# Output by seven half products in four steps of six instead of two, and earlier places for the v loads of the second sequence

## The chip, the cores and the metric

The kernel runs on one core of a Trainium2 chip. The metric is the device time of one execution in microseconds (us); the median of a few runs is compared. The engines of the core are called PE (TensorE), DVE (VectorE), ACT (ScalarE), POOL (GpSimd) and SP (SyncE, which here only issues transfers).

## What is computed

Eight sequences of 3072 tokens with 256 channels go through a gated attention without softmax, and the result through a feed-forward layer that takes the larger of two products:

```python
scores = (1.0 / S) * np.matmul(z, z.transpose(0, 2, 1))   # z: 8 x 3072 x 64
attn = np.maximum(scores, 0.0) ** 2
x = u * np.matmul(attn, v)                                # u, v: 8 x 3072 x 256
h1, h2 = x @ w1, x @ w2                                   # w1, w2: 256 x 1024
out = np.maximum(h1, h2) @ w_out                          # w_out: 1024 x 256
```

The scores of a sequence are symmetric, so the kernel computes a block once and lets the transfer engines transpose it for the other use.

## The kernel before

**Steps.** A sequence is cut into six groups of 512 tokens; a step is one group of output tokens. There are 48 steps: step n belongs to sequence b = n // 6 and has the number s = n % 6 in it. `SEVEN`, the constant of the change, is a set of such numbers s.

**One step on PE** is, in order: the output product of the step three before (`put_o`), the products X and Y of attention with v, and among them the four pairs of banks of the first feed-forward product (`put_d`) of the step two before, and scores of steps to come. Attention times v is done with seven products in place of eight (a Strassen-Winograd scheme): X and Y are sums of such products, their operands are sums over score tiles (`es`, made by DVE in `S1` to `S4`) and over v (`lf`, made by DVE in the jobs `fold`). Most matmuls run as two halves of 64 rows next to each other (`halved`, line 99).

**Scores.** A pair of score tiles goes from PE to a relu (mostly ACT, line 276) and a square (ACT, line 282, or DVE, line 284). SP then issues its transposition `aT<-a_sb`, called a turn, so that a later step can use the block from the other side. X of a step reads turned tiles of all earlier steps of the sequence; the last of them are made in the step just before.

**The output product.** `w_out` times g, g being the larger of the two hidden products. It is written here in two ways:

- *Plain* (`add_second`): four blocks of 128 tokens, ten products each of 64 rows twice, 80 matmuls of 64x256. Two copies by ACT (`oc`, line 287), then the store.
- *Seven* (`add_seven`, line 924; for steps with `s in SEVEN`): seven half products of whole rows, 72 matmuls of 128x128. DVE makes three operand tiles and changes one in place (`G3`, `G1`, `G2`, `G4`, each 128x1024) before the product, and adds the parts after it (`oA` to `oF`: four of 128x256, two of 128x512). ACT copies once 128x256 and once 128x512 (`oc0`, `oc1`).

**The order** of every engine is written by the program when it is built. The order of PE is laid out by hand in `work`. For the other engines a list scheduler (`find_orders`) plays the jobs against a table of costs, with due times from PE's order, 24 rounds, and keeps the round that ends PE first; it decides which squares go to ACT or DVE and in what order SP issues the turns, the transposition of u (`uT`) and the stores. So a changed job changes the order of all the engines around it.

**Loads** are issued by POOL in program order, each timed by a place on PE. v comes in six loads of 256 KB per sequence (`add_v`, line 344), two to a pair buffer; there are six pair buffers, and a sequence uses three. `v_at` (line 1541 for sequence 1, line 1544 for the others) gives their places as (step s, us after its start) in the sequence before; `quiet` (line 1477) moves a place that lies in step 3 or later to the next quiet spot of PE's order. Beside the loads, POOL writes small marks (line 95) that order the two halves of a bank.

Of the kernel before, what the change touches and what calls it, by code (L numbers as in the profile page):

```python
# [11 lines left out]
def kernel(  # L12
# [38 lines left out]
    NDIAG = 2  # L51
    PLAIN = 3
    NA, NT, WIDE = 16, 18, 19
    SEVEN = (0, 1)
    SEVEN_FROM, SEVEN_TO = 0, 46
    SPARE_D = (46, 2)
    DIAG_LAG = 8700, 6700
# [177 lines left out]
    class Step:  # L235
        def __init__(self, n, b, s):
# [3 lines left out]
            self.parted = 0 < n < B * NG - LAG + 1  # L240
            self.seven = s in SEVEN and SEVEN_FROM <= n < SEVEN_TO
            self.count = [0] * KD
# [76 lines left out]
    def v_order(b):  # L319
        return [1, 2, 3, 4, 5, 0] if b else list(range(NG))  # L320
# [23 lines left out]
    def add_v(b, g, at):  # L344
        first = v_pair(b, g)[1] == 0
        if first:
            buf(*v_key(b, g), lambda: vpool.tile([P, 2, G, D], bf16, name="v_sb"))

        def fetch(_):
            load(  # L350
                timed=at is not None,
                out=v_tile(b, g),
                in_=v[b].rearrange("(p t) d -> p t d", p=P)[:, ds(g * G, G), :],
            )

        job(
            ("v", b, g),
            {"POOL": 1300},
            fetch,
            new=v_key(b, g) if first else None,  # L360
            uses=[v_key(b, g)],
            after=list(at or ()) + ([] if first else [("v", b, v_order(b)[v_order(b).index(g) - 1])]),
            lag=8000,
        )
# [1104 lines left out]
    def at_step(b, s, us):  # L1469
        return pe_job_at(starts[NG * b + s] + us * 1000)  # L1470
# [6 lines left out]
    def quiet(at):  # L1477
        i = pe_order.index(at[0])
        if pe_at[i] < starts[LAG]:
            return at  # L1480
        found = [key for key in pe_order[i:] if key in QUIET]
        return found[:1] or at
# [32 lines left out]
    def add_z(b, at, turn_at):  # L1515
        def fetch(_):
            load(
                timed=True,
                out=z_sb_0[:, 1 : 1 + NSB, :],
                in_=z[b].rearrange("(p t) d -> p t d", p=P),  # L1520
            )

        def turn_z(_):
            seqs[b].zT = make_zT(z_sb_0)

        job(("z", b), {"POOL": 1800}, fetch, after=at, lag=7500)
        job(("zT", b), {"SP": 3500}, turn_z, deps=[("z", b)], after=turn_at, lag=3500)
# [10 lines left out]
    for b in range(1, B):  # L1538
        if b == 1:
            z_at, zT_at = (2, 6), (3, 2)  # L1540
            v_at = [(3, 16), (4, 4), (4, 9), (4, 14), (5, 0), (5, 4)]
        else:
            z_at, zT_at = (2, 9), (3, 4)
            v_at = [(3, 11), (3, 16), (4, 5), (4, 12), (5, 2), (5, 6)]
        add_z(b, quiet(at_step(b - 1, *z_at)), at_step(b - 1, *zT_at))
        for g, at in zip(v_order(b), v_at):
            add_v(b, g, quiet(at_step(b - 1, *at)))
# [424 lines left out]
```

## Time and profile before

| what | value |
|---|---|
| runs shown | 915.99, 916.46, 918.47 us, median 916.46 us |
| profiled execution | 915.38 us, of which the span is 913.4 us |
| busy: PE, DVE, ACT, POOL | 901.6, 756.3, 665.1, 92.1 us |
| granted TensorE clock, mean | 0.998 |
| moved by transfers | 146.31 MB, mean 160 GB/s |

The span is the time from the first to the last instruction of one execution. Busy times are the union of an engine's instructions. PE means matmuls, PEld the loading of weights, which overlaps them.

### The profile page before, as it was taken

How to read it: one execution, taken by the hardware profiler on the slowest of the kernel's cores; microseconds unless marked ns; L12 is line 12 of the kernel's file. 1: busy time of each engine (PE TensorE's matmuls, PEld its weight loads, DVE VectorE, ACT ScalarE, POOL GpSimd, SP SyncE). 2: the span in 40 equal slices, each digit the busy share in tenths (PEclk: the TensorE clock that was granted, in tenths of full speed). 3: DMA queues.
4: the chain of work that ended last, by engine and by line, in shares of the span. 5: the costliest groups of instructions: out<-in, count | busy, mean ns of one | idle time of the engine just before them, and what ended most of it. 6: DMA issues, size and time to landing. Idle time of an engine off the chain costs nothing.

```text
span 913.4 us, 31836 instructions
## 1 busy us (share of the span) xinstructions
PE 901.6 (99%) x13685; PEld 672.2 (74%) x13685; DVE 756.3 (83%) x1485; ACT 665.1 (73%) x811; POOL 92.1 (10%) x447
## 2 busy tenths in 40 slices
PE   8999799999999999999999999999999999999998
PEld 3367577777777777777777877778777887777775
DVE  6888688898888988889887998779987899888951
ACT  8868687578776778677786777866888568875634
POOL 2101100111001110011100011000100011000000
PEclk9999999999999999999999999999999999999999
DMA  9999999999999999999999999999999999997711
GB/s 155 169 154 176 167 175 185 168 164 191 177 160 163 149 177 173 167 167 160 165 170 177 147 188 156 179 167 162 161 170 160 174 143 181 188 157 114 123 60 70
DMA packets 382909, 146.31 MB, mean 160 GB/s; under 512 B 361264, under 2 KB 362928, under 8 KB 382768
## 3 DMA queue, kind: packets, MB, share of 16 engines
q1 hardware_dynamic: 366208, 114.54, 75.1%
q0 software_dynamic: 16560, 29.74, 24.1%
q8 instruction: 107, 1.75, 0.8%
q14 instruction: 34, 0.28, 0.1%
HBM read 59.77 MB, written 25.17 MB: 93 GB/s over the span
## 4 chain that ended last, share of the span: by engine, by line
PE 93%; ACT 2%; DMA 2%; DVE 1%; issue 0%; POOL 0%; SPq 0%; POOLq 0%; DVEq 0%
PE acc L87 47%; PE s_ps L87 46%; ACT a_sb L276 1%; DMA v_sb<-in_v_dram 1%; DMA aT<-a_sb 1%; ACT a_held L276 0%; DVE es L290 0%; PE zeros L87 0%; ACT g_sb L276 0%; ACT a_sb L282 0%; DVE e L290 0%; DVE a_sb L293 0%; DVE es L293 0%; DVE xT L297 0%; PE tpz_c L130 0%
## 5 line engine op out<-in xcount | busy, mean ns | idle before, releaser
L87 PEld LDWEIGHTS <-v_sb 64*128 64x128 bf16 (+1 forms) x4464 | 307.7, 94 | 81.9 <-POOL mark_sb L95 15.5
L276 ACT ACTIVATE a_sb<-s_ps 128x1024 bf16<-128x1024 f32 x337 | 301.6, 942 | 83.0 <-PE s_ps L87 80.8
L87 PEld LDWEIGHTS <-lf 64*128 64x128 bf16 x3240 | 246.7, 94 | 49.3 <-POOL mark_sb L95 15.5
L87 PE MATMUL acc<-es,v_sb 64*128 64x256 bf16 x2160 | 279.0, 269 | 0.0
L87 PE MATMUL acc<-es,lf 64*128 64x256 bf16 x1080 | 247.6, 269 | 0.0
L87 PE MATMUL acc<-a_sb,lf 64*128 64x256 bf16 x1224 | 227.1, 269 | 0.4 <-DVE e L290 0.4
L284 DVE TENSOR_TENSOR a_sb<-a_sb 128x1024 bf16<-128x1024 bf16 (+1 forms) x209 | 134.6, 655 | 79.0 <-ACT a_sb L276 73.6
L276 ACT ACTIVATE g_sb<-s_ps 128x1024 bf16<-128x1024 f32 x187 | 185.6, 1025 | 10.0 <-PE s_ps L87 9.4
L87 PE MATMUL s_ps<-xT,w_sb 64*128 64x512 bf16 (+1 forms) x1484 | 189.9, 377 | 0.3 <-POOL mark_sb L95 0.3
L87 PE MATMUL acc<-aT,lf 64*128 64x256 bf16 x936 | 174.1, 270 | 3.3 <-DMA aT<-a_sb 3.3
L87 PE MATMUL s_ps<-w_out_sb,g_sb 64*128 64x256 bf16 (+1 forms) x2240 | 145.6, 263 | 0.0
L290 DVE TENSOR_TENSOR e<-e,acc 128x512 f32<-128x512 f32 (+1 forms) x225 | 125.8, 575 | 19.6 <-PE acc L87 10.6
L87 PE MATMUL acc<-a_sb,v_sb 64*128 64x256 bf16 (+1 forms) x1352 | 140.9, 281 | 0.1
L87 PEld LDWEIGHTS <-g_sb 64*128 64x128 bf16 (+1 forms) x2496 | 126.5, 95 | 15.4 <-issue 3.8
L287 ACT COPY o_sb<-s_ps 128x512 f32<-128x512 f32 (+1 forms) x98 | 51.5, 543 | 106.4 <-PE s_ps L87 104.1
L87 PEld LDWEIGHTS <-w_sb 64*128 64x128 bf16 (+1 forms) x1488 | 69.3, 94 | 70.3 <-POOL mark_sb L95 30.0
L87 PE MATMUL s_ps<-zT 64*128 64x512 bf16 (+2 forms) x774 | 117.0, 334 | 0.4 <-DVE zT L131 0.3
L282 ACT ACTIVATE a_sb<-a_sb 128x1024 bf16<-128x1024 bf16 (+1 forms) x129 | 116.0, 921 | 1.3
L290 DVE TENSOR_TENSOR es<-aT 128x1536 bf16<-128x1536 bf16 (+1 forms) x117 | 106.9, 929 | 5.4 <-DMA aT<-a_sb 5.2
L95 POOL MEMSET mark_sb<- 128x1 bf16 x332 | 33.7, 102 | 720.8 <-PE acc L87 410.1
L87 PE MATMUL acc<-aT,v_sb 64*128 64x256 bf16 x936 | 85.1, 270 | 1.6 <-DMA aT<-a_sb 1.6
L293 DVE TENSOR_TENSOR es<-a_sb 128x512 bf16<-128x512 bf16 x198 | 80.1, 417 | 3.0 <-PE acc L87 2.5
(68 smaller groups left out, 724.4 us busy)
## 6 DMA issues: line engine op xcount, KB each, us to landing
out_dram<-o_sb SPq DMA_DIRECT2D x47, 512.0 KB, 5.9
v_sb<-in_v_dram POOLq DMA_DIRECT2D x48, 256.0 KB, 6.1
u_sb<-in_u_dram POOLq DMA_DIRECT2D x48, 256.0 KB, 5.5
aT<-a_sb SPq DMA_TRANSPOSE x230, 4.9
z_sb<-in_z_dram POOLq DMA_DIRECT2D x7, 384.0 KB, 5.1
w_sb<-in_moe_w_dram POOLq DMA_DIRECT2D x2, 512.0 KB, 7.0
uT<-u_sb SPq DMA_TRANSPOSE x48, 4.6
a_sb<-a_sb SPq DMA_TRANSPOSE x45, 5.6
```

What stands on the lines that cost most here:

```text
L87: newest[0] = pin(nc.tensor.matmul(*args, **kw)).ins
L95: ins = pin(nc.gpsimd.memset(mark_sb, 0.0)).ins
L276: pin(nc.scalar.activation(out_ap, in_ap, AF.Relu))
L282: pin(nc.scalar.activation(ap, ap, AF.Square))
L284: pin(nc.vector.tensor_mul(ap, ap, ap))
L287: pin(nc.scalar.copy(out_ap, in_ap) if eng == "ACT" else nc.vector.tensor_copy(out_ap, in_ap))
L290: pin(nc.vector.tensor_add(*args))
L293: pin(nc.vector.tensor_sub(*args))
```

## The change

Two constants are changed; the code is the same.

```diff
-    SEVEN = (0, 1)
+    SEVEN = (0, 1, 2, 4)
     SEVEN_FROM, SEVEN_TO = 0, 46
...
         if b == 1:
             z_at, zT_at = (2, 6), (3, 2)
-            v_at = [(3, 16), (4, 4), (4, 9), (4, 14), (5, 0), (5, 4)]
+            v_at = [(0, 8), (3, 12), (3, 16), (4, 4), (4, 8), (5, 4)]
```

With the first, 31 steps take the output product by seven half products instead of 16: those with s of 0, 1, 2 or 4 and n below 46. The fifteen new ones are steps 2 and 4 of the first sequence, both in the next six, and step 2 of the last.

With the second, the six loads of v for sequence 1 are issued at other places during sequence 0: the first in step 0, behind the load of w2, instead of late in step 3; the second and third together at the place that the first had; the fourth and fifth at the places that the second and third had; the last with the u load of step 6, as before.

## The prediction

> **What bounds the kernel now.** I read the page first, then PE's waits, the chain of waits, and the busy time by stage.
>
> ```profile
> span 913.4 us, 31836 instructions
> PE 901.6 (99%) x13685; PEld 672.2 (74%) x13685; DVE 756.3 (83%) x1485; ACT 665.1 (73%) x811; POOL 92.1 (10%) x447
> ...
> q1 hardware_dynamic: 366208, 114.54, 75.1%
> q0 software_dynamic: 16560, 29.74, 24.1%
> ...
> PE 93%; ACT 2%; DMA 2%; DVE 1%; issue 0%; POOL 0%; SPq 0%; POOLq 0%; DVEq 0%
> ...
> aT<-a_sb SPq DMA_TRANSPOSE x230, 4.9
> ```
>
> PE is busy 99% of the span and is 93% of the chain that ended last. So a shorter stream of matmuls is worth its full length wherever nothing else becomes late. What PE waits for in mid-kernel is short to list (us in total, times, longest):
>
> ```profile
> PE acc L87 <- DMA aT<-a_sb: 4.8, 2, 3.3
> ...
> PE acc L87 <- DVE e L290: 0.4, 1, 0.4
> ```
>
> Both waits lie at the end of sequence 0. From there on only the other engines can make the change cost something. Here is one round of six steps in the steady part (a window runs from one output product to the next, the sixth is left out and is in the sum; columns: length, then busy time of PE, PEld, DVE, ACT, POOL, granted clock, transfers):
>
> ```profile
> 284.69:302.76 18.07, 18.07 (x292) 14.41 (x291) 17.59 (x35) 12.01 (x18) 1.66 (x8) 1.00 0.94 151
> 302.76:320.89 18.13, 18.13 (x294) 14.34 (x296) 17.40 (x35) 13.59 (x19) 2.72 (x10) 1.00 0.92 135
> 320.89:339.69 18.80, 18.80 (x302) 14.09 (x298) 15.38 (x30) 15.41 (x19) 2.39 (x11) 1.00 1.03 196
> 339.69:358.50 18.81, 18.81 (x304) 14.21 (x300) 16.26 (x36) 15.70 (x18) 1.34 (x9) 1.00 1.14 181
> 358.50:377.19 18.69, 18.69 (x304) 14.22 (x302) 15.30 (x30) 15.36 (x21) 1.34 (x9) 1.00 0.90 156
> ...
> sum 110.44, PE 110.44 PEld 84.81 DVE 96.11 ACT 82.58 POOL 11.33; mean PE 18.41 PEld 14.13 DVE 16.02 ACT 13.76 POOL 1.89
> ```
>
> PE never pauses. DVE is within 0.7 us of full in the two windows that carry the seven products of steps 0 and 1 (17.59 of 18.07, 17.40 of 18.13), and PE still does not wait for it there. The other three have 2.5 to 3.4 us of DVE to spare.
>
> **The output product on PE.** The chain shows a plain and a seven product, each with the attention matmuls behind it (start, us, what):
>
> ```profile
> 156.32 4.37 PE s_ps L87 x80
> 160.68 1.97 PE acc L87 x36
> ...
> 174.26 4.12 PE s_ps L87 x72
> 178.38 2.07 PE acc L87 x36
> ```
>
> 72 matmuls take 4.12 us where 80 take 4.37: 0.25 less. The 36 that follow take 0.10 more behind the seven product, where the array goes back from whole rows to halves. So a converted step is worth 0.25 - 0.10 = 0.15 us, and not the tenth of a product that the count of matmuls suggests. Fifteen steps are converted. That of step 2 of sequence 0 comes just ahead of the long wait for a turn and is swallowed by it, which leaves 14 x 0.15 = 2.1 us.
>
> ```profile
> L87 PEld LDWEIGHTS <-gs 128*128 128x128 bf16 x384 | 22.8, 98 | 0.0
> ```
>
> A weight load lasts 98 ns, 72 of them 7.06 us; since the whole seven product takes 4.12 us, these loads run under each other and under matmuls, 57 ns a pair. The Trainium skill's TensorE: Matmul & The Clock Gate, section Back-to-back issue gap, speaks against the change: in a stream of weight load and matmul pairs it gives about 81 ns for a matmul of 128 columns. By that figure 72 matmuls would be an estimated 5.8 us and every conversion a loss; the trace, at 57 ns, disagrees, and the measurement decides.
>
> **What DVE and ACT get.**
>
> ```profile
> L293 DVE TENSOR_TENSOR gs<-g_sb 128x1024 bf16<-128x1024 bf16 x32 | 22.1, 689 | 8.7 <-ACT g_sb L276 8.1
> ...
> L290 DVE TENSOR_TENSOR o_sb<-o_sb,s_ps 128x256 f32<-128x256 f32 x48 | 20.0, 416 | 4.8 <-ACT o_sb L287 4.4
> ...
> L282 ACT ACTIVATE a_sb<-a_sb 128x1024 bf16<-128x1024 bf16 x101 | 105.8, 1059 | 1.3
> ```
>
> ```profile
> 298.42 0.68 DVE L293 TENSOR_TENSOR gs<-g_sb 128x1024 bf16<-128x1024 bf16 x1
> 299.02 0.68 DVE L290 TENSOR_TENSOR o_sb<-o_sb,ot 128x512 f32<-128x512 f32 x1
> 299.62 0.68 DVE L284 TENSOR_TENSOR a_sb<-a_sb 128x1024 bf16<-128x1024 bf16 x1
> ```
>
> Wide operations last 0.69 us in the groups but start 0.60 apart when DVE is full, so 0.60 is their price. A converted step adds four wide ones (`G`) ahead of the product, 2.4 us, and two wide and four of 128x256 (at most 0.42 each) behind it, 1.2 + 1.7 = 2.9: 5.3 us. Two per sequence are 10.6, and DVE would go from 96.11 to 106.7 of 110.4 us. In the order of the built program the list scheduler has answered: 160 wide squares stand on DVE where 192 stood, and 32 more on ACT (nine narrow ones move too). That takes 32 x 0.60 / 7 = 2.7 us per sequence from DVE, leaving 104.0 (94%), and puts 32 x 1.06 / 7 = 4.8 on ACT, which reaches 87.4 (79%); the output copies of ACT hardly change. By window: 302.76 gets the `G` of step 2 (17.40 + 2.4 = 19.8 of 18.13, so 1.7 must leave it: three squares), 320.89 its sums (15.38 + 2.9 = 18.3 of 18.80), 339.69 the `G` of step 4 (18.7 of 18.81), 358.50 its sums (18.2 of 18.69). It fits, with nothing to spare in three windows running. I price what pinches at 0.1 us per sequence, 0.7 in all: it lies between nothing (two nearly full windows cost PE nothing today) and 0.4 per sequence, 2.8 in all, by the one wait for DVE in the list above. SP's turns wait for these squares and X of a later step for the turns; a turn takes 4.9 us in the median, a step 18, and after sequence 0 no wait of PE for a turn is in the list, so a square that ends a microsecond later on ACT is covered.
>
> **The loads.** The end of sequence 0 is where PE stops:
>
> ```profile
> 97.17 0.38 PE L87 MATMUL s_ps<-zT 64*128 64x512 bf16 x2
> 97.38 0.38 PE L87 MATMUL acc<-aT,v_sb 64*128 64x256 bf16 x4
> ...
> 100.30 0.39 PE L87 MATMUL acc<-aT,v_sb 64*128 64x256 bf16 x4 [1.55 <-DMA aT<-a_sb]
> 103.98 0.40 PE L87 MATMUL acc<-aT,lf 64*128 64x256 bf16 x2 [3.29 <-DMA aT<-a_sb]
> 104.15 0.66 PE L87 MATMUL s_ps<-zT 64*128 64x512 bf16 x2
> 104.58 0.66 PE L87 MATMUL acc<-aT,v_sb 64*128 64x256 bf16 x4
> ...
> 107.14 0.41 PE L87 MATMUL acc<-aT,v_sb 64*128 64x256 bf16 x4
> ```
>
> It waits 1.55 and 3.29 us, 4.84 together, and then runs at half speed: the score pair that took 0.21 us (97.17 to 97.38) takes 0.43 (104.15 to 104.58), until about 107.1. Half of those 3.0 us is 1.5 more, so the stop costs 6.3 us. Why the turn is late:
>
> ```profile
> 87.14 0.53 POOL L108 DMA_DIRECT2D v_sb<-in_v_dram  x1 [0.78 <-PE acc L87]
> 90.33 0.53 POOL L108 DMA_DIRECT2D v_sb<-in_v_dram  x1 [0.97 <-PE s_ps L87]
> ```
>
> ```profile
> 89.80 11.43 SPq L104 DMA_TRANSPOSE aT<-a_sb  x4
> ```
>
> ```profile
> 94.99 8.95 DMA aT<-a_sb
> ...
> 108.28 11.29 DMA v_sb<-in_v_dram
> ```
>
> The turn issued at 94.99 lands 8.95 us later, where the median is 4.9; four turns hold SP for 11.43 us, because two v loads are on the same 16 engines. I price work there by section 3: the load queue has 24.1% of 913.4 us for 29.74 MB, 7.40 us per MB, 1.94 us for a load of 256 KB; SP's queue 75.1% for 114.54 MB, 5.99 per MB, 1.57 for a turn of the same size. The change takes the load at 90.33 away and puts one more at the front of this stretch, beside the first; and the built order of SP has eleven transpositions between that of z and the first store where ten stood, because one turn falls back behind the load of step 0. If the queue drains in between, the late turn lands 1.94 - 1.57 = 0.4 earlier; if not, the extra load in front counts as well and it lands 1.6 later; if it is the load at 90.33 alone that spoils it, 4.05 earlier (8.95 to 4.9). I take the first, which lies between the other two. The load in step 0 costs nothing itself: its buffer is free, POOL is busy 10%, behind it stand only loads needed a step later; its 1.94 us among the turns is the price already counted.
>
> ```profile
> 107.24 0.53 POOL L108 DMA_DIRECT2D v_sb<-in_v_dram  x1 [0.72 <-PE acc L87]
> ...
> 109.26 0.53 POOL L108 DMA_DIRECT2D u_sb<-in_u_dram  x1 [0.45 <-PE acc L87]
> ```
>
> From 107 to 109 two v loads and one of u go out together; the second of v, issued at 108.28, lands after 11.29 us, and DVE's `fold` waits for it, which comes out as PE's wait of 0.4. After the change one of the two is gone: 0.4 saved.
>
> **The sum.** -2.1 - 0.4 - 0.4 + 0.7 = -2.2 us: the span goes from 913.4 to 911.2, and that execution from 915.38 to 913.2. The median of the runs is 1.08 above it: 916.46 - 2.2 = 914.3 us. No change is what lies within 0.3%, 2.75 us, about what a measurement of this kernel can tell; so the likeliest case is a gain near the edge of that. Its own range takes the unknowns: 15 x 0.25 = 3.75 in place of 2.1 if the way back to halves is free, DVE between 0 and 2.8 in place of 0.7, the turn up to 1.6 later in place of 0.4 earlier: -2.2 - 1.65 - 0.7 = -4.5 to -2.2 + 2.1 + 2.0 = +1.9, that is 912 to 918.4.
>
> **Rivals.**
>
> *The stop goes (faster).* The load at 90.33 is what delays the turn. It then lands 4.05 us earlier, the wait shrinks to 0.8 and is too short to halve the speed: 4.05 + 1.5 = 5.6 in place of 0.4, in all -7.4: 909. For it: the turn's 8.95 against 4.9, with that load in flight. Against: the extra turn and the extra load in front, on a stretch where SP hands out turns back to back. The Trainium skill's DMA: Bandwidth & Descriptors, section Issuing engines are not separate DMA queues, says that transfers of all issuing engines share the same 16 and interleave; by it moving a load only moves its price along the queue, which agrees with the 0.4.
>
> *DVE becomes the bound (slower).* In the window at 302.76 the `G` of step 2 meets the sums of step 1. If the squares cannot leave just there, 1.7 us too much stays, Y's sums come late and PE waits for them in each of seven sequences: 11.7; if half can, 5.8: 914.3 + 5.8 = 920. It decides once DVE has no idle time from 302.76 to 358.50. For it: 94%, three windows at the brim. Against: the squares did move, and 97% of a window costs nothing today.
>
> *The weight loads set the pace (slower).* At 98 ns each the seven product would be 7.06 us, +2.7 per step, 15 x 2.7 = 40: 955. The measured 4.12 all but excludes it.
>
> *The change does not do what it says.* The built order has 240 fewer PE instructions, 15 x 2 x 8, so the products are exchanged.
>
> **Chances.** Likeliest case 0.50, of which 0.17 more than 2.75 us faster and 0.33 within; the stop goes 0.28; DVE 0.19; weight loads 0.01; the change does nothing 0.02. Faster 0.17 + 0.28 = 0.45, same 0.33 + 0.02 = 0.35, slower 0.19 + 0.01 = 0.20. The range of 908.5 to 919 leaves out the lower part of the second case and the upper of the third.
>
> **What would show it.** Right: 31 products of 72 matmuls at 4.12 us in the chain, with PE's waits after sequence 0 under 1 us; still a stop before 104 us on `aT<-a_sb` of 4 to 6 us; no wait for `fold` in the next step; DVE near 756 + 15 x 5.3 - 19 = 816 us busy, ACT near 665 + 34 = 699. Wrong: no such stop (second case), or waits of PE for `es` or `e` in every sequence (third). It would be refuted as a whole by a seven product longer than 4.3 us.

## The result, and the profile after

| | runs | median (range), us | before beside it | ratio, 95% interval |
|---|---|---|---|---|
| the whole change | 6 | 910.34 (907.76 to 913.53) | 916.99 | 0.9934 [0.9909, 0.9959] |
| the whole change again, beside the experiments | 12 | 911.32 (907.69 to 916.32) | 916.32 | 0.9960 [0.9935, 0.9984] |

The change makes the kernel faster, by 5 to 6.6 us in the medians. Forecast were 2.2. The time lies inside the range given, 3 to 4 us under the value, and under the 912 at which the likeliest case ended. The kernel before was run 109 more times beside the experiments.

The profiled execution after took 907.76 us, of which the span is 905.9. It is the second shortest of the 18 runs, while that of before, 915.38, is nearer the middle of its own (37 of 109 are shorter). So the 7.6 us between the two profiles are more than the change is worth, which matters below. Here are the lines of the page after that answer to those of before:

```profile
span 905.9 us, 31722 instructions
PE 898.3 (99%) x13565; PEld 673.1 (74%) x13565; DVE 811.1 (90%) x1594; ACT 687.6 (76%) x852; POOL 89.0 (10%) x417
...
q1 hardware_dynamic: 366208, 114.54, 74.4%
q0 software_dynamic: 16560, 29.74, 22.5%
...
PE 94%; ACT 2%; DVE 2%; issue 1%; DMA 0%; POOL 0%; POOLq 0%; DVEq 0%
...
aT<-a_sb SPq DMA_TRANSPOSE x230, 4.4
```

PE is still the bound, at 99% and 94% of the chain. DVE has gained 54.8 us of work and ACT 22.5. The share of DMA in the chain has gone from 2% to 0, and the median turn lands after 4.4 us in place of 4.9; the same bytes take 74.4 and 22.5% of the 16 engines' time where they took 75.1 and 24.1. That fits transfers that met each other less. The waits of PE say what that was (us in total, times, longest):

```profile
PE s_ps L87 <- ACT g_sb L276: 0.9, 1, 0.9
PE acc L87 <- DVE es L290: 0.4, 1, 0.4
```

The 4.8 us on `aT<-a_sb` and the 0.4 on `e` are gone from this execution. Two waits on ACT and DVE have come, 1.3 together, and both lie in sequence 0 (at 106.02 and 87.34 us). No other mid-kernel wait is longer than 0.3. The output products in the chain (start, us, what):

```profile
113.57 4.37 PE s_ps L87 x80
132.37 4.13 PE s_ps L87 x72
150.94 4.37 PE s_ps L87 x80
155.30 1.97 PE acc L87 x36
...
168.87 4.13 PE s_ps L87 x72
173.00 2.07 PE acc L87 x36
```

The product at 132.37 is that of step 4, now with 72 matmuls. The rows that answer to 156.32 and 174.26 of before stand at 150.94 and 168.87: at this point 5.4 us are gained, all of it ahead of the first converted step of the second sequence. The remaining 2.1 us of the 7.5 between the spans come later. One round of the steady part, cut as in the prediction (length, busy time of PE, PEld, DVE, ACT, POOL, granted clock, transfers):

```profile
278.99:296.91 17.92, 17.92 (x292) 14.10 (x290) 17.70 (x35) 12.02 (x17) 1.66 (x8) 1.00 1.13 161
296.91:315.04 18.13, 18.13 (x292) 14.16 (x292) 17.03 (x34) 13.60 (x19) 2.72 (x10) 1.00 0.91 156
315.04:333.81 18.77, 18.77 (x294) 14.71 (x294) 17.70 (x35) 17.37 (x21) 2.19 (x9) 1.00 0.98 159
333.81:352.61 18.80, 18.80 (x301) 14.02 (x296) 18.06 (x39) 15.87 (x20) 1.34 (x9) 1.00 1.08 181
352.61:371.18 18.57, 18.57 (x297) 14.54 (x298) 17.62 (x37) 16.48 (x23) 1.14 (x7) 1.00 0.96 147
...
sum 110.12, PE 110.12 PEld 85.04 DVE 102.91 ACT 86.18 POOL 10.92; mean PE 18.35 PEld 14.17 DVE 17.15 ACT 14.36 POOL 1.82
```

PE never pauses, and the round is 110.12 in place of 110.44: 0.32 for its two converted steps. DVE is at 102.91 of 110.12 (93%) and is waited for nowhere. And the stretch in which PE stopped before:

```profile
91.00:96.00 5.00, 5.00 (x91) 4.49 (x88) 4.69 (x10) 5.00 (x7) 0.00 (x0) 1.00 1.24 147
96.00:101.00 5.00, 5.00 (x79) 3.88 (x78) 4.54 (x12) 3.93 (x7) 0.20 (x2) 1.00 1.06 255
101.00:106.00 5.00, 4.10 (x52) 2.54 (x49) 5.00 (x10) 5.00 (x7) 1.26 (x4) 1.00 1.31 138
106.00:111.00 5.00, 4.84 (x70) 3.81 (x71) 4.75 (x12) 4.16 (x5) 0.20 (x2) 1.00 1.19 214
```

The clock stays at 1.00. PE loses 0.9 us from 101 to 106, where DVE and ACT are full: with the stop gone, these two are what comes last. The queue of SP shows one thing that is earlier, in before (first fence) and after (second):

```profile
40.24 10.76 SPq L104 DMA_TRANSPOSE aT<-a_sb  x3
```

```profile
37.81 6.63 SPq L104 DMA_TRANSPOSE aT<-a_sb  x3
...
84.98 10.52 SPq L104 DMA_TRANSPOSE aT<-a_sb  x4
```

Before, three turns go out together with the load of w_out (issued at 41.02) and hold SP for 10.76 us. After, they go out 2.4 us sooner, take 6.63, and SP keeps that lead: the four turns that were issued from 89.80 on are issued from 84.98 on. Whether the new places of the loads do this, the conversions, or the luck of one execution, the two profiles can't tell.

### The profile page after: what moved, and what is told of

Its sections match the earlier page's. It is cut to its first block, busy times and chain, and to the rows that moved or that the text cites. A ratio compares the mean times of both kernels' runs of the same rounds, so it can differ in the third digit from the quotient of the medians.

```text
span 905.9 us, 31722 instructions
## 1 busy us (share of the span) xinstructions
PE 898.3 (99%) x13565; PEld 673.1 (74%) x13565; DVE 811.1 (90%) x1594; ACT 687.6 (76%) x852; POOL 89.0 (10%) x417
## 3 DMA queue, kind: packets, MB, share of 16 engines
q1 hardware_dynamic: 366208, 114.54, 74.4%
q0 software_dynamic: 16560, 29.74, 22.5%
## 4 chain that ended last, share of the span: by engine, by line
PE 94%; ACT 2%; DVE 2%; issue 1%; DMA 0%; POOL 0%; POOLq 0%; DVEq 0%
PE acc L87 48%; PE s_ps L87 46%; ACT a_sb L276 1%; DVE es L290 1%; ACT a_held L276 0%; ACT a_sb L282 0%; DVE es L293 0%; DVE o_sb L290 0%; DMA o_sb<-in_z_dram 0%; ACT o_sb L287 0%; DVE e L290 0%; DVE aT L293 0%; DVE xT L297 0%; DVE ot L290 0%; DVE a_sb L293 0%
## 5 line engine op out<-in xcount | busy, mean ns | idle before, releaser
L87 PEld LDWEIGHTS <-v_sb 64*128 64x128 bf16 (+1 forms) x4464 | 311.4, 94 | 80.1 <-POOL mark_sb L95 14.5
L87 PEld LDWEIGHTS <-lf 64*128 64x128 bf16 x3240 | 251.4, 94 | 44.8 <-POOL mark_sb L95 15.5
L282 ACT ACTIVATE a_sb<-a_sb 128x1024 bf16<-128x1024 bf16 (+1 forms) x170 | 153.1, 930 | 0.8
L284 DVE TENSOR_TENSOR a_sb<-a_sb 128x1024 bf16<-128x1024 bf16 (+1 forms) x168 | 111.0, 669 | 29.4 <-ACT a_sb L276 27.9
L87 PEld LDWEIGHTS <-g_sb 64*128 64x128 bf16 (+1 forms) x2016 | 107.8, 96 | 13.0 <-issue 7.0
L287 ACT COPY o_sb<-s_ps 128x256 f32<-128x256 f32 (+1 forms) x98 | 47.1, 516 | 72.7 <-PE s_ps L87 72.7
L95 POOL MEMSET mark_sb<- 128x1 bf16 x302 | 30.7, 102 | 719.3 <-PE acc L87 477.2
L87 PE MATMUL s_ps<-w_out_sb,g_sb 64*128 64x256 bf16 (+1 forms) x1520 | 99.4, 253 | 0.0
```

Of the source, the lines that this page charges most:

```text
L87: newest[0] = pin(nc.tensor.matmul(*args, **kw)).ins
L95: ins = pin(nc.gpsimd.memset(mark_sb, 0.0)).ins
L282: pin(nc.scalar.activation(ap, ap, AF.Square))
L284: pin(nc.vector.tensor_mul(ap, ap, ap))
L287: pin(nc.scalar.copy(out_ap, in_ap) if eng == "ACT" else nc.vector.tensor_copy(out_ap, in_ap))
```

## The experiments

Every kernel ran 12 times unless noted, beside the kernel before on the same chip. The spread is wide, so the table has the mean with its standard error beside the median. The 109 runs of the kernel before have a mean of 916.39 ± 0.25 us (median 916.32, 909.83 to 922.91).

| kernel | median, us | ratio, 95% interval | mean, us |
|---|---|---|---|
| conversions alone | 912.19 | 0.9947 [0.9919, 0.9975] | 912.35 ± 0.91 |
| loads alone | 916.04 | 0.9998 [0.9969, 1.0027] | 916.77 ± 1.08 |
| the first load alone | 917.79 | 1.0027 [0.9998, 1.0056] | 918.66 ± 1.13 |
| the other loads alone | 915.18 | 0.9984 [0.9955, 1.0012] | 914.86 ± 0.87 |
| 13 late conversions | 911.03 | 0.9955 [0.9928, 0.9981] | 911.42 ± 0.92 |
| 2 early conversions | 916.24 | 0.9993 [0.9963, 1.0022] | 915.92 ± 0.89 |
| conversions, the other loads | 912.11 | 0.9955 [0.9929, 0.9981] | 912.38 ± 0.86 |
| order of round 4, nothing else | 916.78 | 0.9988 [0.9962, 1.0013] | 915.53 ± 0.95 |
| 13 late conversions, old order in sequence 0 | 913.55 | 0.9974 [0.9953, 0.9995] | 913.74 ± 0.58 |
| five of six, late (6 runs) | 932.61 | 1.0177 [1.0137, 1.0218] | 932.77 ± 1.67 |
| the whole change in sequence 0 alone | 916.78 | 0.9994 [0.9965, 1.0024] | 915.11 ± 1.09 |
| the whole change (18 runs) | 910.74 | (above) | 911.24 ± 0.63 |

The mean of the first load alone leaves out one run of 927.79 us.

**Either half of the change.** *Conversions alone:*

```diff
-    SEVEN = (0, 1)
+    SEVEN = (0, 1, 2, 4)
```

> The new set of steps for the seven half products, with the v loads of the second sequence at their old places. Theory A (the stop at the end of sequence 0 went because of the loads): the stop stays, 4 to 6 us of waits of PE for aT near 100 us with half the speed behind it; only the conversions count, 14 x 0.15 = 2.1 us, and somewhat of that goes into the first sequence where DVE now has more to do: 1 to 2.5 us faster than before, ratio 0.997 to 0.999. Theory B (the other order of DVE and ACT work that comes with the conversions relieves the stop): no such wait, 5 to 7 us faster, ratio 0.992 to 0.995. In both a steady round of six steps takes 110.1 us instead of 110.4.

*Loads alone:*

```diff
-            v_at = [(3, 16), (4, 4), (4, 9), (4, 14), (5, 0), (5, 4)]
+            v_at = [(0, 8), (3, 12), (3, 16), (4, 4), (4, 8), (5, 4)]
```

> The new places of the v loads, with the old set of steps for the seven half products. Theory A (loads): the stop goes, 4 to 6 us faster, ratio 0.993 to 0.996, and a steady round still takes 110.4 us. Theory B (conversions): the stop stays and the time is within 1 us of before.

The conversions bring 912.19, the loads nothing: 916.04. In the trace of the conversions alone (909.95 us) a round takes 110.13 us, as both theories said, and PE waits 1.6 us on `aT<-a_sb`: between the theories, like the time, which is 4.5 us below before (916.72) where A had 1 to 2.5 and B 5 to 7. The waits of PE with the loads alone:

```profile
PE acc L87 <- DMA aT<-a_sb: 5.2, 3, 2.5
```

The sum is as before, but it lies in two places:

```profile
60.06 0.61 PE L87 MATMUL acc<-aT,v_sb 64*128 64x256 bf16 x4 [2.43 <-DMA aT<-a_sb]
...
108.05 0.40 PE L87 MATMUL acc<-aT,lf 64*128 64x256 bf16 x2 [2.51 <-DMA aT<-a_sb]
```

At the end of sequence 0 it is 2.5 us, though the load that stood at 90.33 us is gone; so a turn can be late there without that load. The wait at 60 us is one that the profile of before has not. This execution, 920.68 us, is the second longest of its twelve, and the loads alone also run in another order: the scheduler keeps round 12 of its 24, for the kernel before round 6. So loads and order are not separated by it. SP has no lead here either: in this execution the transposition of w2, issued at 33.19 us ahead of the three turns, held it for 8.31 us, and they went out at 42.95.

**The loads in two parts.** *The first load alone* goes to (0, 8):

```diff
-            v_at = [(3, 16), (4, 4), (4, 9), (4, 14), (5, 0), (5, 4)]
+            v_at = [(0, 8), (4, 4), (4, 9), (4, 14), (5, 0), (5, 4)]
```

> Before, with only the first of the six v loads moved to step 0; the other five stay, the one near 90 us included. Theory A1 (the early load makes one turn fall back in the queue of SP, so that the turns of step 2 go out ahead of the load of w_out near 41 us, and the whole queue of transfers runs some 5 us ahead from there on): the transposition of z is issued near 58 us instead of 63, the stop goes, 4 to 6 us faster. Theory A2 (the load near 90 us delays the awaited turn): that load is still there, the stop stays, within 1.5 us of before.

*The other loads alone*, with the first beside the second:

```diff
-            v_at = [(3, 16), (4, 4), (4, 9), (4, 14), (5, 0), (5, 4)]
+            v_at = [(3, 12), (3, 12), (3, 16), (4, 4), (4, 8), (5, 4)]
```

> Before, with the loads two to six at the new places and the first together with the second late in step 3, so that no load stands in step 0 and none near 90 us. Theory A1 (early load and order of the turns): z is still transposed near 63 us, the stop stays or grows with the third load at 68 us, 0 to 2 us slower than before. Theory A2 (load near 90 us): the awaited turn lands in about 5 us instead of 9, the stop shrinks to 1 us, 4 to 6 us faster.

917.79 and 915.18: neither differs from before by more than its interval, and the early load if anything costs. Theory A2 had the first within 1.5 us of before, and in the medians it is; for the other loads it had 4 to 6 us less and theory A1 0 to 2 more, and neither came. The traced execution of the first load alone is the one of 927.79 us and has 5.3 us of waits on `aT<-a_sb`; that of the other loads took 913.47 us and has 2.8.

**Which conversions pay.** The 13 of the second sequence and later, and the 2 of sequence 0, each with the old loads. Beside `SEVEN = (0, 1, 2, 4)`, in line 241, for the first and for the second:

```diff
-            self.seven = s in SEVEN and SEVEN_FROM <= n < SEVEN_TO
+            self.seven = s in (SEVEN if n >= 6 else (0, 1)) and SEVEN_FROM <= n < SEVEN_TO
```

```diff
-            self.seven = s in SEVEN and SEVEN_FROM <= n < SEVEN_TO
+            self.seven = s in (SEVEN if n < 6 else (0, 1)) and SEVEN_FROM <= n < SEVEN_TO
```

> Old loads; steps 2 and 4 of six are made by seven half products from the second sequence on only (13 steps), the first sequence is as before. Theory C (the 13 steps give 0.155 us each in the traces, and what the seven products gave beyond that comes out of sequence 0's stop): 13 x 0.155 = 2.0 us less than before, about 914.7, with the stop as in the kernel before (PE waits on aT of 3 to 5 us). Rival D (the stop's size is only chance from run to run, and all of the 4.5 us of the seven products alone comes from the steps, some of it outside the profiled run): about 912.2, as with the seven products everywhere.

> Old loads; steps 2 and 4 by seven half products in the first sequence only (2 steps), the rest as before. Theory C: the remainder, 4.5 - 2.0 = 2.5 us less than before, about 914.2, with PE waits on aT shorter than 3 us. Rival D: within 0.5 us of before, about 916.5, since two steps give 0.3 us.

911.03 and 916.24. The late ones alone give what all of them gave, and more than the 2.0 us of theory C, which put the rest down to the early ones: that part of C falls. Rival D gave 912.2 and 916.5 and fits better. But the two kernels differ from before by more than the conversions. With the late ones (a single one in the last sequence is enough) the scheduler keeps round 4 in place of round 6, with the early ones round 5, and in sequence 0 these are other orders of squares and turns. That was the next thing to separate.

**Conversions with the other loads**, and the whole change beside it:

> Seven half products everywhere, and the new load places but for the first, which stands with the second at (3, 12) and not at (0, 8). Theory E (the early load costs about 1 us, as it did alone, 917.79 against 916.72, and the other five gain about 1.5, 915.18): 912.2 - 1.5 = 910.7 or better, no later than the whole change run beside it. Rival F (the early load pays once the seven products are there, by keeping one load out of the stretch from 65 to 109 us): 1 us or more above the whole change.

> The whole change, run beside the other three. Its six runs so far have a median of 910.34, 6.6 below the kernel before. If that was no chance it lies at 910 to 911 again, and if the sum of the parts holds (4.5 for the seven products, nothing for the loads) at 912.2.

912.11 against 911.32: no difference that these runs could show. The trace of this second profiled run of the whole change (909.37 us) has the stop smaller, and not gone:

```profile
PE acc L87 <- DMA aT<-a_sb: 1.6, 2, 0.9
```

Both E and F are within reach; the place of the early load can't be told apart from none.

**Order and conversions, crossed.** *The order of round 4 alone:*

```diff
-    ROUNDS = 24
+    ROUNDS = 5
```

> Nothing of the change; the scheduler stops after its fifth round, so that it keeps the order of round 4 and not that of round 6. PE's order, the transfers by POOL and everything behind sequence 0 stay; in sequence 0 one square of 128x1024 goes from ACT to DVE, one of 128x256 from DVE to ACT, one turn of u goes ahead of a turn of a held tile, and some sums change places. It is the order that the kernel with 13 converted steps (911.03) has in sequence 0. Theory G (what that kernel gained beyond 13 x 0.155 = 2.0 us is the order of sequence 0 that the scheduler happened to keep): 5.0 - 2.0 = 3.0 us less than before, about 913.4. Rival D (the converted steps themselves give all of it): within 0.7 us of before, 916.3 to 916.5.

*The 13 late conversions with the order of round 6*, which is that of before in sequence 0 (beside the edit of line 241):

```diff
-        if best_end is None or pe_jobs[-1].done < best_end:
+        if _ == 6:
```

> Steps 2 and 4 by seven half products from the second sequence on (13 steps), with the order of round 6 kept, which in sequence 0 is the order of the kernel before, instruction for instruction on every engine. Theory G: 13 x 0.155 = 2.0 us less than before, about 914.4, and PE's waits on aT in sequence 0 as in the kernel before (4 to 5 us). Rival D: about 911.3, as with the 13 steps and the other order.

The order alone has a median 0.6 us above that of before beside it, and a mean 0.9 ± 1.0 below. That is not the 3.0 of theory G. The 13 conversions with the old order give 2.6 in the medians, near G's 2.0 and about half of D's 5. In that trace the stop stands where it stood, 3.25 us of it at 101 and 104 us:

```profile
PE acc L87 <- DMA aT<-a_sb: 3.9, 3, 2.1
```

```profile
283.96 4.13 PE s_ps L87 x72
...
394.10 4.12 PE s_ps L87 x72
```

From output product to output product, six steps later, it is 110.14 us, in place of 110.44: the same 0.30 as in the whole change. So neither G nor D holds whole. The order of round 4 in place of that of round 6 is worth 0.9 ± 1.0 us in the means without the 13 conversions and 2.3 ± 1.1 with them: it may give something, but these runs don't show how much.

**More conversions.** Steps 0 to 4 of six, late (with the first of the two edits of line 241), with the old loads:

```diff
-    SEVEN = (0, 1)
+    SEVEN = (0, 1, 2, 3, 4)
```

> From the second sequence on five steps of six by seven half products (0 to 4), so 7 more than in the kernel with 13 new ones. If PE stays the bound, each gives 0.155 us once more, 1.1 us less than that kernel beside the same order of sequence 0. If DVE becomes the bound (5.3 us more per step brings it from 94 to about 99 per cent of a round), PE waits on DVE in every round and the time is 1 us or more above that kernel's 911, up to 917.

932.61 us: far worse than either expectation. The page and the waits of PE:

```profile
span 935.0 us, 31648 instructions
PE 907.9 (97%) x13525; PEld 681.6 (73%) x13525; DVE 818.3 (88%) x1619; ACT 712.2 (76%) x877; POOL 88.0 (9%) x407
...
PE 62%; DVE 20%; DMA 11%; issue 5%; ACT 1%; SPq 1%; POOL 1%; DVEq 0%; POOLq 0%; ACTq 0%
```

```profile
PE acc L87 <- DVE es L290: 7.8, 6, 1.3
...
PE acc L87 <- DVE e L290: 2.4, 5, 0.8
```

```profile
sum 114.00, PE 111.87 PEld 86.93 DVE 105.06 ACT 90.98 POOL 10.73; mean PE 18.64 PEld 14.49 DVE 17.51 ACT 15.16 POOL 1.79
```

The last row is a stretch of 114 us from 243 on, not a round. The span is 27.4 us over that of the 13 late conversions (907.6). The last plain product of sequence 0 starts at 158.05 us here and at 152.13 there, so 5.9 of it lie in sequence 0, where both have the same products; the other 21.5 us are 3.1 per sequence. PE now waits for `es` six times, 1.3 us each, and runs thinner where it counts as busy: 907.9 us for 13525 matmuls, where the change has 898.3 for 13565. The chain, which was PE to 94%, goes through DVE for 20% and through transfers for 11%. DVE's share of the span is 88%, no more than with the 13 late conversions (802.7 of 907.6 us), and in the stretch it is 92% (105.06 of 114): as a share of a longer time, it hides that DVE is now part of the bound. The chain also goes on through others:

```profile
316.25 0.28 issue
316.53 8.34 DMA v_sb<-in_v_dram
324.87 0.03 issue
...
324.97 0.44 DVE lf L290
```

Here the chain waits 8.34 us for a load of v before DVE can make `lf`.

**The whole change in sequence 0 alone**, in the order that it has there; from the second sequence on as before (the edits are against the whole change):

```diff
-    ROUNDS = 24
+    ROUNDS = 5
...
-            self.seven = s in SEVEN and SEVEN_FROM <= n < SEVEN_TO
+            self.seven = s in (SEVEN if n < 6 else (0, 1)) and SEVEN_FROM <= n < SEVEN_TO
```

> The whole change in sequence 0 alone: the new load places, and steps 2 and 4 by seven half products there; from the second sequence on the output products are as in the kernel before. The scheduler stops after its fifth round, and so keeps the order that the whole change has; in sequence 0 it is that order instruction for instruction on every engine. Theory H (the whole change is a sum of two: 13 steps at 0.155 = 2.0 us, and an order of sequence 0, with loads and turns in it, in which PE's stop is mostly gone): 5.0 (911.3 against 916.3) - 2.0 = 3.0 us less than before, about 913.4, and the granted clock is 0.999 or 1.0 in at least half of the runs, as with the whole change (13 of 18) and unlike the kernel before (7 of 92). Rival I (sequence 0 gives nothing without the later steps, as the order of round 4 alone gave next to nothing): 916 to 917, the clock as before.

The median is 916.78, as rival I said; the mean 915.11 ± 1.09; but the clock is 0.999 or 1.0 in 7 of 12 runs, as theory H said. The runs fall into two heaps, 910.2 to 914.7 (5 runs) and 916.4 to 920.5 (7). The profiled one belongs to the first:

```profile
113.61 4.37 PE s_ps L87 x80
```

```profile
168.91 4.13 PE s_ps L87 x72
```

These rows stand at 113.57 and 168.87 in the profile of the whole change: to 0.04 us the same sequence 0, with no stop. Its span, 908.6, is 2.7 above the 905.9 of the whole change, of which 13 conversions of 0.16 make 2.1. So in its good executions this sequence 0 does what the profile of the change shows; in others the same program is 6 to 10 us slower, and two of those have a clock of 0.999, so that it is not the halved speed in every case. Neither H nor I holds whole: what the change does to sequence 0 shifts the odds at most.

## Why the prediction was right or wrong

**What the 13 conversions are worth.** In four pairs of kernels, one has the 13 late conversions and the other has not, with the same loads and the same order of sequence 0. Their means differ by

| pair | difference, us |
|---|---|
| old order, old loads | 2.7 ± 0.6 |
| order of round 4, old loads | 4.1 ± 1.3 |
| early conversions, old loads | 3.6 ± 1.3 |
| the whole change in sequence 0 | 3.9 ± 1.3 |

Weighted, that is 3.2 ± 0.5. Every trace shows 0.30 to 0.32 per round of two, 2.0 to 2.1 for all. The other 1.1 is a little over two standard errors; whether it is chance or lies in executions that were not traced stays open.

The traces do say where the rest is. The last plain product of sequence 0 starts at 156.32 us before and at 150.94 after. From there to the end of the span, six traces with the 13 conversions (two of them of the whole change) take 755.0 to 755.7 us, and five without them 757.0 to 757.6: 2.0 apart. Up to there the same eleven range from 150.9 to 159.7 us. The loads alone and the first load alone have 759.0 and 759.7 behind it, each with one stop of PE (1.3 and 1.9 us) for which the profile shows no cause. So in traced executions the conversions bring 2.0 us, and nearly all of what differs beyond that lies in sequence 0.

**What sequence 0 is worth.** By itself 1.3 ± 1.1 us. The whole change is 5.15 ± 0.7 below before in the means; less 3.2, that leaves 2.0 ± 0.8, less the traced 2.1 it leaves 3.0. So something comes from sequence 0, between one and three us, and not the 5.4 that the two profiles show there: those put one of the best executions of after beside a middling one of before.

That the range holds the time is in part luck. It was drawn wide enough to take in most of the case "the stop goes", while the sum itself, 2.2 us, was right in its first term and missed what sequence 0 gives.

The steps of the prediction:

- **A converted step is worth 0.15: right.** 4.13 for 72 matmuls beside 4.37 for 80, 2.07 beside 1.97 behind them; 0.16 per step by the round. The 81 ns for such a matmul that the Trainium skill gives (TensorE: Matmul & The Clock Gate, section Back-to-back issue gap) would have made each of them an estimated 5.8 us; at 57 ns (4.13 / 72) the 15 new ones are as short as the 16 old.
- **DVE and ACT: right in size.** Priced were 104.0 and 87.4 us per round, measured 102.91 and 86.18; 816 and 699 in all, measured 811.1 and 687.6. The seven sequences pay nothing for it where 0.7 was priced. The place was wrong: the 1.3 us that PE does wait for ACT and DVE lie in sequence 0, for which no price was made. The rival "DVE becomes the bound" needed the squares to stay; with two conversions per sequence they moved. With three, more of them moved (ACT has 161 wide squares, with the 13 late conversions 130), and PE waits for DVE all the same (932.61 us).
- **The stop stays: this step failed.** The prediction expected waits of 4 to 6 us on `aT<-a_sb` before 104 us. The profile after has none of them, the other profiled run of the change 1.6 us. The result is that of the rival "the stop goes", 909, but not by its mechanism: it took the load at 90.33 as the cause, and the loads alone leave 2.5 us of waits at the end of sequence 0, 5.2 in all, and 916.04 us. The step was also wrong in kind. It priced one stop from one execution to a tenth of a microsecond, when its size differs from execution to execution of the same program; 0.4 or 4.05 earlier were both readings of a single draw. The rule of the Trainium skill (DMA: Bandwidth & Descriptors, section Issuing engines are not separate DMA queues) is that transfers of all issuing engines run on the same 16 engines and interleave. If a moved load then only moves its price, as the prediction took it, the loads alone should change nothing, and they stand at 0.9998 of before.
- **The loads: -0.4 for `fold`, unsupported.** The wait on `e` is gone from the first profile after the change, but also from the trace of the 13 late conversions with the old order, which has the old loads; and in the other profiled run of the change it is there, 0.6 us at 108.47. It comes and goes with the execution.
- **Step 2 of sequence 0 gives nothing: not contradicted.** The two early conversions together gave 0.5 ± 0.9.

## What to carry to other kernels

A gain that repeats in every step can be worked out from one profile to a few hundredths and holds. A stop that depends on transfers meeting each other can't: it is one draw, and its size, its cause and what removes it need many executions, not one trace. Where a program schedules itself, compare with the kept order held fixed, since an edit in the last sequence can change the first. And an engine at 93% may cost nothing while one more conversion per round, meant to bring 1.1 us in all, cost 21: DVE's work rose by 15.6 us in all, 2.2 per sequence, and its share of the span not at all. Count the work per round, not its share of the span.

## What was not expected of the hardware

The spread of one and the same program, and how well its granted clock tells it. Runs of the kernel before, by the mean clock that each shows:

| mean clock | runs | mean time, us |
|---|---|---|
| 0.999 or 1.0 | 8 | 911.5 |
| 0.998 | 30 | 914.8 |
| 0.996 or 0.997 | 54 | 916.8 |
| 0.994 or less | 17 | 920.1 |

The long wait of PE in the prediction's rows is followed by half speed, so in the main a low clock tells of long stops. The whole change is at 0.999 or more in 13 of its 18 runs, before in 8 of 109, the conversions alone in 3 of 12, the loads alone in 3 of 12. But it doesn't take both halves: the 13 late conversions have it in 6 of 12, the conversions with the other loads in 7 of 12, the whole change in sequence 0 alone in 7 of 12. The order may have a part in it: that of round 4 has 4 of 12 where before has 8 of 109, and with the 13 late conversions 6 of 12 where the old order has 1. No trace shows why, and it stays open.
